# Attention scores as two products of 64 keys each, in a fused linear-attention and MLP kernel

## The chip, the cores and the metric

The kernel runs on one core of a Trainium2 chip. The core has five engines that run side by side: TensorE (PE; its weight loads are shown apart as PEld), VectorE (DVE), ScalarE (ACT), GpSimd (POOL) and SyncE (SP), which issues the DMAs here. The metric is the device time of one execution in microseconds, the median over runs; less is better.

## The reference, cut to what matters

A recurrence over 768 steps for 4 batches and 8 heads of width 48 with a complex, elementwise decay, and behind it a GELU MLP over all 3072 tokens:

```python
mag = np.sqrt(a_re * a_re + a_im * a_im)
scale = np.minimum(mag, 0.999) / (mag + 1e-06)
for t in range(S):
    new_re = ar * S_re - ai * S_im
    new_im = ar * S_im + ai * S_re
    S_re, S_im = (new_re + k_t v_t^T, new_im)
    y[:, :, t] = q_t @ S_re
...
h = x @ w_in            # 384 -> 2048
g = gelu(h)
return g @ w_out        # 2048 -> 384
```

## The kernel before, in words

**Lanes.** The products of the decays are made by a scan on DVE over 24 slices in four groups of positions (`GROUPS`: two of 2 x 64 positions, two of 2 x 128). Each slice is normalised (ACT and DVE, with `ident_r` sums on PE in the first slices), scanned (`tt`, `bt`), multiplied into k and q (`xt<-a,bt`) and written to DRAM (`kq<-xt`). A unit can load its part (`kqn<-kq`) when all slices of its group are written.

**Units.** There are 24 units of 128 positions of one batch, position by position: units 0 to 3 and 4 to 7 lie in the groups with chunks of 64 rows, units 8 to 23 in those with 128. A unit transposes k and q of four heads at a time (a half: `att<-ident_r,kqn`, copied to `kT` and `qT`), makes their scores (`scores`: `att<-qT,kp`, `kT` being the upper part of a `kp` tile), multiplies the scores by a causal mask on DVE (`kp<-att,causal`; for chunks of 64 the mask also blocks the earlier chunk), and makes `y` from them (`att<-kp,vn`), from the state before (`att<-qT,st`), and adds k^T v to the state (`att<-vn,kqn`). Then `x` and `xT` are split into a high and a low part (`minus`) and moved by DMA (`xT<-x`).

**Weights.** The weights come in 32 pieces as 64-bit floats (`raw`) and are converted to a high and a low part: on ACT and DVE (`wh`), and three products on PE (`po<-wh,ident_r`, then two with `minus`).

**Blocks.** Two or three units form one of nine blocks. Per block and each of 16 slices of the hidden width, `first` makes `ph` (nine products), ACT takes the GELU twice (`gf`, `gh`), DVE the difference (`gl`), and `second` adds to `po`.

**Order.** All of this is written to a list of steps, and a planner (`Plan`) puts every engine's instructions in one fixed order by estimated costs and by seven constants, `MORE`, which shift the priority of the kinds of work (lanes of each group, weights, units, blocks). Every instruction is then issued from line 393, so the groups of the profile are told apart by their tiles. PE products of 32-bit floats appear as two records in the trace, those with float32r operands as one.

`att` are three PSUM banks that transposes, scores and `y` take in turn.

Of the kernel before, what the change touches and what calls it, by code (L numbers as in the profile page):

```python
# [23 lines left out]
C = 128  # L24
# [36 lines left out]
def vap(t, dims):  # L61
    t = t[:] if not isinstance(t, bass.AP) else t
    return bass.AP(t.tensor, t.offset, [list(t.ap[0])] + dims)
# [28 lines left out]
N_A = 4  # L92
WL = 0.307

MORE = dict(lanes0=80.88, lanes1=16.18, lanes2=-95.71, lanes3=203.18, weights=-3.78, units=92.04, blocks=48.05)
BIAS = dict(vector=0.45, scalar=-0.29, gpsimd=0.38)


# [9 lines left out]
class Plan:  # L108
# [142 lines left out]
    def natural(self):  # L251
# [4 lines left out]
        for i in range(len(steps) - 1, -1, -1):  # L256
# [9 lines left out]
            rest[i] = t  # L266
        return [t + MORE[s.kind] for t, s in zip(rest, steps)]

# [135 lines left out]
def lanes_and_chunks(ctx, tc, flags, a_lanes, x_lanes, v_units, w_in, w_out, out):  # L404
    nc = tc.nc
# [4 lines left out]
    P = Plan(nc, loose=[flags])  # L410

    def ring(name, shape, n, dtype=F32, pool=cst):
        return itertools.cycle([pool.tile(shape, dtype, name=f"{name}{i}", tag=f"{name}{i}")[:] for i in range(n)])
# [44 lines left out]
    own = [ps.tile([128, 512], F32, name=f"att{i}", tag=f"att{i}")[:] for i in range(3)]  # L458
    ph = [ps.tile([128, 512], F32, name=f"ph{i}", tag=f"ph{i}")[:] for i in range(2)]
    pos = [ps.tile([128, 512], F32, name=f"po{i}", tag=f"po{i}")[:] for i in range(BLK)]  # L460
    ps_h = itertools.cycle(ph)
    raws = ring("raw", [128, DM * (2 if wide else 1)], N_RAW, w_in.dtype)
    whs = ring("wh", [128, DM], 2, U32)
# [277 lines left out]
    def unit(u):  # L741
# [3 lines left out]
        chunks, row = [], 0  # L745
# [80 lines left out]
        qT, kT, kp, pm = [], [], [], []  # L826
# [13 lines left out]
        def scores(hh):  # L840
            p = next(ps_att)
            with P.together():
                for j in range(4):
                    P.tensor.matmul(out=p[:, j * 128:(j + 1) * 128], lhsT=kT[hh][:, j, :], rhs=qT[hh][:, j, :], start=True, stop=True)
            t = kp[hh]
            P.vector.tensor_tensor(out=t, in0=p.rearrange("p (j l) -> p j l", j=4), in1=vap(masks[chunks[0][4]], [[0, 4], [1, 128]]), op=ALU.mult)
            pm.append(t)
# [17 lines left out]
        if early:  # L865
# [6 lines left out]
            for hh in range(2):  # L872
                turn(kn, kT, "kT", hh)
                turn(qn, qT, "qT", hh)
                scores(hh)
                y(hh)
                for c in with_state:
                    y_state(c, hh)
            for c in with_state:
                add_state(c, turned[c])  # L880
        else:
            for hh in range(2):
                turn(kn, kT, "kT", hh)
                turn(qn, qT, "qT", hh)
                scores(hh)
# [12 lines left out]
        j = next(j for j in range(len(BLOCKS)) if u < first_unit[j + 1])  # L898
# [238 lines left out]
def tile_complex_linear_attention_moe(ctx, tc, q, k, v, a_re, a_im, w_in, w_out, a_lanes, x_lanes, v_units, w_pieces, out):  # L1137
# [9 lines left out]
    with ExitStack() as fast:  # L1147
        fast.enter_context(tc.manual_schedule())
        lanes_and_chunks(fast, tc, flags, a_lanes, x_lanes, v_units, w_pieces, w_out, out)
# [81 lines left out]
```

## Time and profile before

| | before |
|---|---|
| median of 3 runs | 715.82 us (715.65 to 717.05) |
| span of the profiled execution | 713.3 us; the median run is 2.5 us longer |
| PE busy | 654.8 us (92%), 5190 matmul records |
| PE weight loads | 595.6 us (84%) |
| DVE, ACT, POOL busy | 456.6, 451.0, 52.6 us |
| chain that ended last, by engine | PE 65%, DVE 12%, ACT 11%, DMA 7% |

The span runs from the first to the last instruction; the time of a run holds some us around it. Busy times are sums of one engine's instructions, averaged over stages in which different engines wait for each other. PE's records overlap, so its work is read here from the start of one group to the start of the next.

### The profile page before, as it was taken

Reading aid. Unit: us, or ns where it says so; the run is one execution under the profiler, and the core shown is the slowest. Engines: PE = TensorE matmul, PEld = TensorE weight load, DVE = VectorE, ACT = ScalarE, POOL = GpSimd, SP = SyncE. Lnnn points to the kernel's source line nnn. Section 1 sums busy time; section 2 is a strip of 40 time slices with the busy share of each in tenths; the row PEclk is TensorE's granted clock in tenths of the full one; section 3 lists DMA queues with packets and bytes.
Section 4 is the critical chain, followed back from the end, with each engine's and each line's share of the span. In section 5 each row is a group of like instructions: output and inputs, shape, how many; then the busy total and the mean of one; then the engine's idle time right before and its main releaser. Section 6 shows DMA issues by size and latency. Waiting matters only on the chain.

```text
span 713.3 us, 13809 instructions
## 1 busy us (share of the span) xinstructions
PE 654.8 (92%) x5190; PEld 595.6 (84%) x5190; DVE 456.6 (64%) x1104; ACT 451.0 (63%) x1069; POOL 52.6 (7%) x85
## 2 busy tenths in 40 slices
PE   5635699997999999999999999999999999999995
PEld 2312478886889899989899999999999999999995
DVE  5999989997899999989999962433232221222211
ACT  8777779997688778887898864353433343343332
POOL 1002241003000200301010000100000000000000
PEclk9975599999999999999999999999999999999998
DMA  9357977668275566657586465032302112010000
GB/s 300 108 132 189 241 192 226 166 175 181 48 215 132 122 145 168 158 160 198 160 249 156 93 168 145 26 91 68 103 10 74 61 40 64 1 40 6 23 1 26
DMA packets 112840, 86.68 MB, mean 122 GB/s; under 512 B 55808, under 2 KB 105088, under 8 KB 112768
## 3 DMA queue, kind: packets, MB, share of 16 engines
q1 hardware_dynamic: 112768, 85.75, 44.9%
q8 instruction: 42, 0.69, 0.4%
q14 instruction: 30, 0.25, 0.1%
HBM read 56.82 MB, written 23.59 MB: 113 GB/s over the span
## 4 chain that ended last, share of the span: by engine, by line
PE 65%; DVE 12%; ACT 11%; DMA 7%; SPq 2%; issue 2%; DVEq 0%; ACTq 0%
PE po L393 23%; PE ph L393 23%; PE att L393 19%; DVE a L393 3%; DMA m<-st 3%; SPq L393 2%; ACT a L393 2%; ACT tab L393 2%; ACT wh L393 2%; DMA kqn<-kq 2%; DVE tt L393 2%; DVE tab L393 1%; DVE xt L393 1%; ACT L391 1%; DMA xt<-in_x_lanes_dram 1%
## 5 line engine op out<-in xcount | busy, mean ns | idle before, releaser
L393 PE MATMUL ph<-xT,wi_hi 128*128 128x384 f32 (+1 forms) x864 | 211.5, 326 | 0.0
L393 DVE TENSOR_TENSOR gl<-gf,gh 128x384 fp32r<-128x384 f32 (+1 forms) x141 | 72.2, 512 | 168.0 <-ACT gf L393 165.1
L393 PEld LDWEIGHTS ph<-xT,wi_hi 128*128 128x128 f32 x864 | 153.1, 189 | 3.6 <-issue 1.6
L393 ACT ACTIVATE gh<-ph 128x384 fp32r<-128x384 f32 (+1 forms) x144 | 65.7, 456 | 129.4 <-PE ph L393 129.1
L393 PE MATMUL ph<-xT,wi_lo 128*128 128x384 f32 (+1 forms) x432 | 137.5, 318 | 0.0
L393 PE MATMUL po<-wo_hi,gh 128*128 128x384 f32 x384 | 132.9, 346 | 1.7 <-ACT gh L393 1.4
L393 PE MATMUL po<-wo_lo,gh 128*128 128x384 f32 x384 | 129.8, 338 | 0.0
L393 PE MATMUL po<-wo_hi,gl 128*128 128x384 f32 x384 | 93.8, 345 | 0.0
L393 PEld LDWEIGHTS ph<-xT,wi_lo 128*128 128x128 f32 x432 | 81.7, 189 | 0.0
L393 PEld LDWEIGHTS po<-wo_hi,gh 128*128 128x128 f32 x384 | 72.2, 188 | 5.0 <-ACT gh L393 3.4
L393 PEld LDWEIGHTS po<-wo_lo,gh 128*128 128x128 f32 x384 | 72.5, 189 | 0.1
L393 DVE TENSOR_TENSOR tt<-bt,a 128x192 f32<-128x192 f32 x192 | 68.3, 356 | 1.2
L393 PEld LDWEIGHTS po<-wo_hi,gl 128*128 128x128 f32 x384 | 65.4, 189 | 1.6 <-issue 0.9
L393 ACT ACTIVATE gf<-ph 128x384 f32<-128x384 f32 (+1 forms) x144 | 65.3, 453 | 0.7 <-DVE gl L393 0.5
L393 PE MATMUL att<-qT,kp 96*128 96x128 f32 x384 | 52.2, 279 | 1.5 <-DVE kp L393 1.5
L393 PEld LDWEIGHTS att<-qT,kp 96*128 96x128 f32 x384 | 48.4, 192 | 3.8 <-ACT a L393 2.1
L393 DVE TENSOR_TENSOR bt<-tt 128x96 f32<-128x96 f32 x192 | 49.2, 256 | 1.1
L393 PE MATMUL po<-wh,ident_r 128*128 128x384 f32 x64 | 33.7, 615 | 15.5 <-DVE wh L393 6.9
L393 DVE TENSOR_TENSOR kp<-att,causal 128x512 f32<-128x512 f32 x48 | 33.0, 687 | 19.0 <-PE att L393 18.1
L393 PE MATMUL att<-ident_r,kqn 128*96 128x128 f32 x384 | 38.5, 240 | 5.2 <-DMA kqn<-kq 4.4
L393 ACT COPY kp<-att 96x512 f32<-96x512 f32 x47 | 27.3, 582 | 24.4 <-PE att L393 23.8
L393 PEld LDWEIGHTS att<-ident_r,kqn 128*96 128x96 f32 x384 | 33.9, 128 | 9.3 <-issue 5.6
(177 smaller groups left out, 1018.1 us busy)
## 6 DMA issues: line engine op xcount, KB each, us to landing
kqn<-kq SPq DMA_DIRECT2D x16, 768.0 KB, 5.4
xt<-in_x_lanes_dram SPq DMA_DIRECT2D x24, 384.0 KB, 4.5
kq<-xt SPq DMA_DIRECT2D x24, 384.0 KB, 4.1
kq<-xt SPq DMA_DIRECT2D x48, 192.0 KB, 4.5
a<-in_a_lanes_dram SPq DMA_DIRECT2D x20, 384.0 KB, 3.3
raw<-in_w_pieces_dram SPq DMA_DIRECT2D x16, 384.0 KB, 4.1
raw<-in_moe_w_out_dram SPq DMA_DIRECT2D x16, 384.0 KB, 4.5
vn<-in_v_units_dram SPq DMA_DIRECT2D x24, 256.0 KB, 5.1
```

What stands on the lines that cost most here:

```text
L391: self.nc.scalar.preload_act_table_set(table)
L393: getattr(getattr(self.nc, engine), name)(*args, **kw)
```

## The change

The four 128 x 128 score products of a half become eight: for each head the keys 0 to 63 against all queries of the chunk and the keys 64 to 127 against the queries 64 to 127. For chunks of 64 rows the lower keys meet the queries 0 to 63 alone. The part of the bank that is no longer written is masked to zero afterwards; so that it holds finite numbers the three `att` banks are cleared at the start. Four of the seven planner constants are moved by more than 1.

```diff
-MORE = dict(lanes0=80.88, lanes1=16.18, lanes2=-95.71, lanes3=203.18, weights=-3.78, units=92.04, blocks=48.05)
+MORE = dict(lanes0=60.85, lanes1=16.18, lanes2=-77.98, lanes3=203.18, weights=-44.11, units=115.14, blocks=47.55)
...
     pos = [ps.tile([128, 512], F32, name=f"po{i}", tag=f"po{i}")[:] for i in range(BLK)]
+    for p in own:
+        nc.vector.memset(p, 0.0)
...
                 for j in range(4):
-                    P.tensor.matmul(out=p[:, j * 128:(j + 1) * 128], lhsT=kT[hh][:, j, :], rhs=qT[hh][:, j, :], start=True, stop=True)
+                    for k0 in (0, 64):
+                        k1 = k0 + 64 if k0 or chunks[0][4] == 64 else C
+                        P.tensor.matmul(out=p[k0:k0 + 64, j * 128 + k0:j * 128 + k1], lhsT=kT[hh][:, j, k0:k0 + 64],
+                                        rhs=qT[hh][:, j, k0:k1], start=True, stop=True)
```

In the planner a product with at most 64 stationary columns has the form "narrow", with a cost of its own and a cost for changes of form, so the scores change their form there, too.

PE's order at unit 20, before: the first half's scores (four products of 128 x 128), then transposes of the second half, and later the second half's scores and the first `y`.

```order
L393 MATMUL ph_112<-xT_149,wi_lo 128x384
L393 MATMUL att_108<-qT_144,kp_146 128x128 x4
L393 MATMUL att_109<-ident_r,kqn_139 96x128 x4
L393 MATMUL att_110<-ident_r,kqn_139 96x128 x4
L393 MATMUL ph_112<-xT_149,wi_hi 128x384 x2
...
L393 MATMUL po_115<-wo_lo,gh_155 128x384
L393 MATMUL att_108<-qT_145,kp_147 128x128 x4
L393 MATMUL att_109<-kp_146,vn_141 64x128 x4
L393 MATMUL po_113<-wo_hi,gl_157 128x384
```

The same place of the change, where each "..." inside a half stands for the pair of rows above it, three times more:

```order
L393 MATMUL po_115<-wo_lo,gh_159 128x384
L393 MATMUL att_108<-qT_147,kp_149 64x128
L393 MATMUL att_108<-qT_147,kp_149 64x64
...
L393 MATMUL att_109<-ident_r,kqn_142 96x128 x4
L393 MATMUL att_110<-ident_r,kqn_142 96x128 x4
L393 MATMUL po_113<-wo_hi,gl_161 128x384
...
L393 MATMUL ph_112<-xT_152,wi_lo 128x384
L393 MATMUL att_108<-qT_148,kp_150 64x128
L393 MATMUL att_108<-qT_148,kp_150 64x64
...
L393 MATMUL att_109<-kp_149,vn_144 64x128 x4
L393 MATMUL ph_112<-xT_152,wi_hi 128x384 x2
```

The first half's scores are now a group of their own with 64 stationary columns between groups with 128 and 96; the second half's are joined to the `y` product that has 64 as well.

SP's order (DMA issues) around the first loads of units 4 and 5, before: `raw` are weight pieces, `kq` the last writes of group 1, `kqn` the units' loads, each "x2" the two chunks of 64 rows.

```order
L393 DMA raw_118<-in_w_pieces_dram 128x768
L393 DMA raw_119<-in_moe_w_out_dram 128x768
L393 DMA a_125<-in_a_lanes_dram 128x2x384
L393 DMA kq_105<-xt_131 64x8x192
L393 DMA kq_105<-xt_131 64x8x96 x2
L393 DMA kq_105<-xt_132 64x8x192
L393 DMA kq_105<-xt_132 64x8x96 x2
L393 DMA xT_149<-x_150 16x256 x6
L393 DMA xt_131<-in_x_lanes_dram 128x8x96
L393 DMA kqn_139<-kq_105 64x8x192 x2
L393 DMA kqn_140<-kq_105 64x8x192 x2
```

And in the change:

```order
L393 DMA kq_105<-xt_135 64x8x192
L393 DMA kq_105<-xt_135 64x8x96 x2
L393 DMA vn_145<-in_v_units_dram 128x512
L393 DMA raw_121<-in_w_pieces_dram 128x768
L393 DMA raw_122<-in_moe_w_out_dram 128x768
L393 DMA kqn_142<-kq_105 64x8x192 x2
L393 DMA kqn_143<-kq_105 64x8x192 x2
L393 DMA raw_119<-in_w_pieces_dram 128x768
L393 DMA xT_152<-x_153 16x256 x4
L393 DMA raw_120<-in_moe_w_out_dram 128x768
```

The loads of units 4 and 5 had all 32 weight pieces ahead of them; four pieces stand behind them now.

## Rows read from the trace of the kernel before

**Rows 1.** The page's head and PE's line of its busy times: busy us (share of the span) x instructions.
```profile
span 713.3 us, 13809 instructions
...
PE 654.8 (92%) x5190; PEld 595.6 (84%) x5190; DVE 456.6 (64%) x1104; ACT 451.0 (63%) x1069; POOL 52.6 (7%) x85
```

**Rows 2.** Busy time of each engine in four stages: stretch, its length, busy us (x instructions) by engine, then granted clock of TensorE, DMA share and GB/s.
```profile
core 0: us, PE busy (x) PEld busy (x) DVE busy (x) ACT busy (x) POOL busy (x), PEclk, DMA share, GB/s
0.00:85.00 85.00, 44.71 (x97) 22.49 (x99) 73.28 (x201) 64.65 (x158) 8.80 (x30) 0.77 0.70 194
85.00:175.00 90.00, 84.56 (x802) 71.85 (x800) 82.41 (x210) 81.71 (x213) 19.66 (x19) 0.97 0.71 188
175.00:425.00 250.00, 244.99 (x2153) 227.74 (x2154) 230.13 (x558) 199.40 (x416) 20.42 (x26) 0.99 0.61 155
425.00:640.00 215.00, 215.00 (x1666) 209.28 (x1664) 56.97 (x102) 82.87 (x216) 3.74 (x11) 1.00 0.21 62
```

**Rows 3.** PE's waits between 175 and 425 us: who waited for whom, us in total, times, longest.
```profile
PE att L393 <- DMA kqn<-kq: 4.4, 1, 4.4
PE att L393 <- DVE kp L393: 2.7, 4, 1.0
PE att L393 <- ACT kp L393: 0.8, 1, 0.8
```

**Rows 4.** PE in order of time around a half's scores that stand between full-array groups (unit 18): start us, us, engine, line, operation, out<-in, stationary rows*columns, shape, count of records.
```profile
502.49 0.52 PE L393 MATMUL ph<-xT,wi_hi 128*128 128x384 f32 x2
502.84 0.34 PE L393 MATMUL ph<-xT,wi_lo 128*128 128x384 f32 x1
...
503.54 1.05 PE L393 MATMUL att<-qT,kp 96*128 96x128 f32 x8
504.35 0.77 PE L393 MATMUL att<-ident_r,kqn 128*96 128x128 f32 x8
504.95 0.58 PE L393 MATMUL ph<-xT,wi_hi 128*128 128x384 f32 x2
505.37 0.33 PE L393 MATMUL ph<-xT,wi_lo 128*128 128x384 f32 x1
```

**Rows 5.** The same view at unit 20's `y` and state products, which have 64 and 48 stationary columns.
```profile
558.75 0.66 PE L393 MATMUL att<-kp,vn 128*64 128x128 f32 x8
559.34 0.78 PE L393 MATMUL po<-wo_hi,gl 128*128 128x384 f32 x3
...
560.30 0.34 PE L393 MATMUL ph<-xT,wi_lo 128*128 128x384 f32 x1
560.57 0.66 PE L393 MATMUL att<-kp,vn 128*64 128x128 f32 x8
561.06 1.05 PE L393 MATMUL att<-qT,st 96*48 96x128 f32 x16
562.03 0.62 PE L393 MATMUL ph<-xT,wi_hi 128*128 128x384 f32 x2
562.49 0.34 PE L393 MATMUL ph<-xT,wi_lo 128*128 128x384 f32 x1
562.67 0.34 PE L393 MATMUL po<-wo_hi,gh 128*128 128x384 f32 x1
```

**Rows 6.** The same view at state products with 64 moving columns.
```profile
232.38 0.65 PE L393 MATMUL att<-qT,st 96*48 96x64 f32 x16
232.97 0.62 PE L393 MATMUL ph<-xT,wi_hi 128*128 128x384 f32 x2
```

**Rows 7.** Instructions that read or write `kp`: count, duration in ns as min/median/max, first and last start, forms.
```profile
L393 PE MATMUL att<-qT,kp x384: 272/275/488, 89.8 to 639.1; 96*128 96x128 f32 x192
...
L393 PE MATMUL att<-kp,vn x352: 271/273/324, 112.2 to 640.8; 128*64 128x128 f32 x176
L393 DVE TENSOR_TENSOR kp<-att,causal x48: 672/691/693, 91.1 to 639.5; 128x512 f32<-128x512 f32 x48
```

**Rows 8.** PE in order of time: a weight piece (three groups, the first and the last shown by their starts) and the start of unit 4; in brackets the idle time before and its releaser.
```profile
160.62 0.81 PE L393 MATMUL po<-wh,ident_r 128*128 128x384 f32 x2
...
161.62 0.51 PE L393 MATMUL po<-wo_hi,gl 128*128 128x384 f32 x2
161.97 0.40 PE L393 MATMUL ph<-xT,wi_hi 128*128 128x256 f32 x2
...
176.15 1.06 PE L393 MATMUL att<-ident_r,kqn 128*96 128x128 f32 x8 [4.39 <-DMA kqn<-kq]
```

**Rows 9.** Busy time from 85 to 175 us of the instructions that read or write `wh` alone: length, PE, PEld, DVE, ACT (x instructions), clock, DMA share, GB/s. A piece has two such records on PE, three instructions on DVE and five on ACT.
```profile
85.00:175.00 90.00, 14.59 (x34) 5.63 (x34) 23.59 (x51) 29.36 (x82) 0.97 0.71 188
```

**Rows 10.** SP's DMA issues in order of time ahead of unit 4's load.
```profile
156.83 7.07 SPq L393 DMA_DIRECT2D kq<-xt  x6
164.01 4.28 SPq L393 DMA_DIRECT2D xT<-x  x6
...
168.97 2.66 SPq L393 DMA_DIRECT2D kqn<-kq  x4
```

**Rows 11.** DVE's first instruction.
```profile
6.65 0.36 DVE L393 TENSOR_SCALAR wh<-raw 128x384 uint32<-128x384 uint32 x1 [6.65 <-ACT wh L393]
```

**Rows 12.** All engines in order of time, of which the load and the first transposes of unit 8.
```profile
301.33 1.00 SPq L393 DMA_DIRECT2D kqn<-kq  x2
...
308.29 0.69 PE L393 MATMUL att<-ident_r,kqn 128*96 128x128 f32 x8
```

**Rows 13.** A row of the page's DMA issues: count, KB each, median us from issue to landing.
```profile
kqn<-kq SPq DMA_DIRECT2D x16, 768.0 KB, 5.4
```

## The prediction

> **What bounds the kernel now.** I read the stages first. Up to 85 us no engine carries the kernel: PE works off weight pieces while the lanes of group 0 run on DVE and ACT. From 85 to 175 us three engines are near full: PE 84.56, DVE 82.41 and ACT 81.71 of 90 us [rows 2]. From 175 to 425 PE has 244.99 of 250, DVE 230.13; from 425 to 640 PE has 215.00 of 215 at a granted clock of 1.00, and DVE and ACT are mostly idle [rows 2]. A busy PE could still be a waiting one, so I read its waits next: between 175 and 425 us they are 4.4 us for `kqn<-kq`, 2.7 for DVE and 0.8 for ACT, and nothing else of size [rows 3]. So from unit 4's first transposes at 176.15 [rows 8] PE works through its order without a pause for the remaining 537 us of the span of 713.3 [rows 1]. What the change does to the sum of PE's pitches (from the start of one group to the start of the next) reaches the end, less what happens before 176 us.
>
> **What PE pays now for scores.** A half is eight full-array records. It starts at 503.54, the transposes behind it at 504.35: 0.81 us. The records overlap with what follows, and the next group pays for it: the transposes take 0.60 to 504.95. A plain transpose run costs 0.53 to 0.54 (0.60 less the 0.07 to 0.08 that any group pays behind such a run: `ph` x2 takes 0.42 at 504.95 where it takes 0.35 at 502.49) [rows 4]. So a half costs 0.81 + 0.08 = 0.89, and 48 halves cost 42.7 us.
>
> **What a 64-column product costs.** Products with 64 or fewer stationary columns are in the program already (`att<-kp,vn`, `att<-qT,st`). Sixteen records, eight products, with 128 moving columns take 561.06 to 562.03, 0.97 us; 0.10 of it is the way out (below), so 0.87 / 8 = 0.109 each [rows 5]. With 64 moving columns eight products take 232.38 to 232.97, 0.59; less 0.05 in and 0.10 out, 0.055 each [rows 6].
>
> **What a run of them costs besides.** Going into one, `ph` x1 takes 0.27 (560.30 to 560.57) and not 0.18 (562.49 to 562.67): +0.09. The first four products take 0.49, where four in the middle take 0.44: +0.05. Four that end the run take 0.59 (558.75 to 559.34) and not 0.49: +0.10. The `ph` x2 behind it takes 0.46 (562.03 to 562.49) and not the 0.35 of rows 4: +0.11 [rows 5, 4]. The toll is 0.35 us for each run, however short.
>
> **How many runs.** I counted them in both orders, a run being neighbours on PE with at most 64 stationary columns. Before there are 60, the scores among none of them. After there are 86: 20 consist of scores alone, 28 mix scores with `y` or state products. Transpose runs go from 63 to 73. The example of unit 20 shows it: scores that stood between full-array groups at no toll become two runs of their own kind, one alone, one joined to `kp,vn`. The 26 added runs cost 26 x 0.35 = 9.1 us, ten transpose runs 10 x 0.08 = 0.8.
>
> **What the new products cost.** The eight units with 64-row chunks (16 halves) get 64 x 64 products: 8 x 0.055 = 0.44 a half, 7.0 us. The other 32 halves have, per head, one product of 128 moving columns for the lower key half and one of 64 for the upper. No row shows such an unequal pair. Lower bound: they take their 0.109 and 0.055 one behind the other, 4 x 0.164 = 0.66 a half. Upper bound: the longer product of each pair sets the pace. The rows say something on this. A record of `att<-kp,vn` lasts 273 ns, a full-array record of `att<-qT,kp` 275 [rows 7]. A narrow record is therefore no quicker than a full one; eight full ones take 0.81 us, and sixteen narrow ones 0.87. That is two narrow ones in the time of one, side by side. Wherever this kernel issues them, they alternate between the lower and the upper output half (`h % 2 * 64`, `c0`) with equal lengths. If the two halves of the output are what runs side by side, a lower product of 128 beside an upper one of 64 leaves the upper half idle, and a head costs two equal products, 2 x 0.109: 4 x 0.218 = 0.87 a half. I take 0.87, because the equal record times are what side by side looks like and a cheaper product isn't.
>
> The Trainium skill, page TensorEngine Tiling (Array Packing), section Key Properties, says that different tiles of the array can load weights and multiply in parallel. No run here shows an unequal pair; by that rule the upper bound would hold, and the sum would be the one I take, where by the products' own rows added up it would be the lower bound's.
>
> **The sum on PE.** After: 7.0 + 32 x 0.87 + 9.1 + 0.8 = 44.7 against 42.7, +2.1 us with the fractions kept. With 0.66 for the wide halves: 7.0 + 21.1 + 9.1 + 0.8 = 38.0, -4.7.
>
> **The stage before 176 us.** The three memsets on DVE write 128 x 512 PSUM words each; the nearest row, a DVE pass over such a bank, takes 0.69 [rows 7], together 2.1 at most. DVE's first instruction of before starts at 6.65 after 6.65 of waiting [rows 11]: free; without that cover 2.1. The new table moves weight pieces behind the lanes of group 1. In SP's order the four `kqn` loads of units 4 and 5 have no piece behind them before, and four `raw` loads after; on PE 31 of the 32 pieces stand ahead of unit 4's first transposes before, 26 after. A piece takes 1.0 us of PE (160.62 to 161.62) [rows 8]; on ACT 29.36 us over some 16.5 pieces, 1.8, and on DVE 23.59 over 17, 1.4, without the casts of `lo` [rows 9]. Five fewer pieces take 8.9 off ACT and 6.9 off DVE, the two engines on which the lanes of group 1 run, and both are nearly full there. I let unit 4's `kqn` land 9 us earlier than the 176 of before. PE has 5.0 less in pieces ahead of it, four fewer groups each of block 0's `ph`, `wo_hi,gh` and `wo_lo,gh` and two fewer `gl` (3.2, at 0.175 per 384 columns, from 161.62 to 161.97 for two) [rows 8], and about 1.5 less for the eight halves of units 0 to 3 (7.1 before; 3.5 and six tolls after): 9.7. PE so arrives 9.7 earlier for a load that comes 9 earlier, and the wait of 4.4 becomes about 5. I take +1.0, with bounds of -4.4 (the pieces kept for later fill the wait) and +4.4 (the lanes gain half of it only). `kqn` in turn waits behind `kq<-xt` and the `xT<-x` on SP, 156.83 to 168.97 [rows 10]; the new order has two `raw` loads there and no `xT<-x`, which I cost at nothing, since the wait is for `kq` to land.
>
> Pieces moved behind 176 us add 7 to DVE in a stage where it has 230 of 250: still under its room of 20, so PE stays the bound. **Sum:** 713.3 + 2.1 + 1.0 = 716.4 span. The median run of 715.82 is 2.5 longer than the span shown; I keep that: **718.9**.
>
> **Rivals.**
> *Narrow products are simply cheaper.* The wide halves cost 0.66, PE's sum falls by 4.7, and with the +1.0 ahead the time is 715.8 - 3.7 = 712.1, faster. For it: the two prices of rows 5 and 6 follow moving columns exactly (0.109 and 0.055). Against: the equal record times of rows 7. It decides from a wide half under 0.78 on (41.7, which is 42.7 less the 1.0, = 7.0 + 9.9 + 32 x 0.775).
> *The wait at unit 4 closes.* The pieces left over give PE work while `kqn` lands; 4.4 goes and the +1.0 with it: 718.9 - 5.4 = 713.5. For it: five pieces of 1.0 are there to fill it. Against: PE takes its order as it stands, and the pieces stand behind the transposes.
> *A later unit waits.* Unit 8's `kqn` is issued at 301.33, a load takes 5.4 to land, and its transposes start at 308.29 [rows 12, 13]: about 1 us to spare. If the lanes of group 2 come later than that against PE, a wait of the kind of rows 8 appears: up to 4.4, giving 723.3.
>
> **Chances.** The forecast 0.45, cheaper products 0.22, the closed wait 0.13, the later wait 0.20. A change under 0.2% (1.4 us) can't be told from none in this kernel. Faster by more: 0.22 and over half of 0.13, 0.30; within: 0.17, from the low edge of the forecast and the rest of the closed wait; slower: 0.53. The range, 710.5 to 723.5, takes in cheaper products and the later wait; cheaper products with the wait closed too (706.7) lie outside. The forecast's own range is 717 to 721.
>
> **What would show it.** In the changed kernel a wide half with its 16 records should take about 0.87 us to the next group within a run, and 64 x 64 halves 0.44; 0.66 for the wide ones proves me wrong. Waits of PE behind 175 us should stay under 10 us, with one at unit 4 near 167 us. The stage from 425 us to the end, where PE alone counts, should hold more PE time per unit than before. The forecast fails if the wide half is cheap, if the wait for `kqn` goes, or if DVE becomes PE's releaser between 175 and 425.

## The result and the profile after

| | before | changed |
|---|---|---|
| median | 716.43 us (715.65 to 717.19, 4 runs) | 726.98 us (720.77 to 730.44, 4 runs) |
| ratio, 95% interval | | 1.0142 (1.0104 to 1.0180) |
| span of the profiled execution | 713.3 us | 725.7 us (its time: 727.38) |

The change is slower by 10.5 us. The direction was forecast, the size was not: 718.9 was the forecast, 723.5 the upper end of the range. Where a run was disturbed the comparison leaves it out, so a ratio below can differ from that of the medians beside it.

The head of the page of the changed kernel:

```profile
span 725.7 us, 14647 instructions
...
PE 660.7 (91%) x5574; PEld 589.3 (81%) x5574; DVE 458.8 (63%) x1099; ACT 456.4 (63%) x1090; POOL 70.8 (10%) x95
```

The four stages of [rows 2], with the same columns (busy us of PE, PEld, DVE, ACT, POOL; granted clock, DMA share, GB/s):

```profile
0.00:85.00 85.00, 44.03 (x118) 22.98 (x118) 76.20 (x209) 64.37 (x157) 7.03 (x29) 0.73 0.70 196
85.00:175.00 90.00, 83.27 (x857) 69.43 (x856) 75.10 (x189) 74.78 (x191) 17.99 (x18) 0.89 0.73 183
175.00:425.00 250.00, 240.40 (x2294) 217.63 (x2290) 232.68 (x561) 204.13 (x443) 40.57 (x37) 0.99 0.61 154
425.00:640.00 215.00, 215.00 (x1744) 203.61 (x1743) 58.34 (x106) 85.75 (x219) 5.17 (x12) 1.00 0.22 62
```

Two rows stand out against [rows 2]. From 85 to 175 us the granted clock fell from 0.97 to 0.89. From 175 to 425 us PE has 4.6 us less busy time. The last stage is as full as before. DVE and ACT have 7 us less busy time from 85 to 175 us, but that is work that went elsewhere: the weight pieces (`wh`) alone take 8.0 us less of DVE and 6.6 less of ACT there than in [rows 9]:

```profile
85.00:175.00 90.00, 11.30 (x24) 4.15 (x24) 15.64 (x37) 22.73 (x62) 0.89 0.73 183
```

A busy PE hides two things, so I took PE's records apart: for each kernel the sum of all pitches (start to next start) at full clock, which is PE's **work**; the time in which no record ran, **idle**; and what the half clock added, which is half of PE's running time where the granted clock is 0.50. Counted is from unit 0's first transposes to PE's last record, cut at unit 4's first transposes:

| us | unit 0 / unit 4 at | to unit 4: work, idle, half clock | from unit 4: work, idle, half clock |
|---|---|---|---|
| before | 86.3 / 176.2 | 81.7, 6.6, 1.6 | 522.8, 4.8, 2.7 |
| changed | 85.2 / 170.1 | 69.9, 6.7, 8.3 | 535.7, 10.6, 2.5 |

PE's whole work rose by 1.1 us (604.5 to 605.6). The loss is elsewhere: 5.9 us of idle time and 6.6 of half clock. With the 1.1 of work, and less 1.1 by which unit 0 came earlier, they make the 12.4 us of the span.

Not all of the half clock lies behind the two stops below. Of the 8.3 us, 3.8 stand ahead of 94 us, where the clock comes to full at 93.7 us and not at 89.4 as before (1.6 us there). The stretch from 89 to 94 us, changed first:

```profile
89.00:94.00 5.00, 5.00 (x33) 3.81 (x32) 3.84 (x7) 2.47 (x6) 0.00 (x0) 0.53 0.79 241
```
```profile
89.00:94.00 5.00, 5.00 (x63) 4.30 (x61) 3.64 (x9) 4.23 (x10) 0.00 (x0) 0.96 1.03 292
```

All traces with the order of the change have this late rise, at 93.5 to 96.6 us, also those of kernels that lost nothing; no run was made on it.

**The products** cost about what the forecast took. PE in order of time, a wide half by itself (start, us, engine, line, operation, out<-in, stationary rows*columns, shape of the first record, count of records):

```profile
353.22 0.34 PE L393 MATMUL ph<-xT,wi_lo 128*128 128x384 f32 x1
353.49 1.09 PE L393 MATMUL att<-qT,kp 96*64 96x128 f32 x16
354.50 0.62 PE L393 MATMUL ph<-xT,wi_hi 128*128 128x384 f32 x2
354.96 0.33 PE L393 MATMUL ph<-xT,wi_lo 128*128 128x384 f32 x1
...
102.94 0.66 PE L393 MATMUL ph<-kp,vn 128*64 128x128 f32 x8
103.42 0.64 PE L393 MATMUL att<-qT,kp 96*64 96x64 f32 x16
103.89 0.39 PE L393 MATMUL ph<-qT,st 96*48 96x64 f32 x8
```

From 353.49 to 354.50 are 1.01 us: 0.87 within rounding, and the 0.15 that a run of narrow products pays inside it; `ph` x2 behind it takes the 0.46 of [rows 5]. The short half between other narrow products takes 0.47, where 0.44 was forecast.

**The first stop.** PE around 116 us (the bracket is the idle time ahead and its releaser), then the granted clock (third figure from the end of a row) in pieces of 2 us:

```profile
115.52 0.81 PE L393 MATMUL att<-m,other_half 96*128 96x384 f32 x2
118.77 0.77 PE L393 MATMUL ph<-xT,wi_hi 128*128 128x256 f32 x2 [2.44 <-DMA xT<-x]
```
```profile
116.00:118.00 2.00, 0.33 (x2) 0.00 (x0) 1.99 (x7) 1.97 (x6) 0.00 (x0) 0.89 0.44 154
118.00:120.00 2.00, 1.23 (x6) 1.26 (x7) 2.00 (x8) 0.59 (x2) 1.33 (x1) 0.50 0.20 37
120.00:122.00 2.00, 2.00 (x23) 1.63 (x22) 0.64 (x3) 0.00 (x0) 1.49 (x1) 0.50 0.96 286
122.00:124.00 2.00, 2.00 (x35) 1.91 (x33) 0.00 (x0) 1.32 (x6) 0.00 (x0) 0.50 0.23 91
...
128.00:130.00 2.00, 2.00 (x30) 1.71 (x28) 1.18 (x3) 1.42 (x4) 0.00 (x0) 1.00 0.10 25
```

PE waits 2.4 us for the DMAs of `xT`, the clock falls to 0.50 (1.2 GHz) for some 10 us, and PE's products take about double there: `ph` x2 0.77 us where it took 0.40 in [rows 8]. DVE and ACT stop with it (DVE 0.00 busy from 122 to 124 us), because copies of PE's results stand at the head of their queues. Their waits from 115 to 130 us (who for whom, us, times, longest):

```profile
DVE xT L393 <- PE att L393: 5.4, 1, 5.4
```
```profile
ACT xT L393 <- PE att L393: 3.5, 1, 3.5
```

The same 15 us of both kernels, changed first:

```profile
115.00:130.00 15.00, 12.55 (x104) 10.35 (x103) 8.73 (x26) 8.97 (x24) 2.82 (x1) 0.66 0.47 142
```
```profile
115.00:130.00 15.00, 15.00 (x175) 12.41 (x173) 14.78 (x41) 14.17 (x42) 1.05 (x1) 1.00 0.62 188
```

DVE and ACT have 6.1 and 5.2 us less busy time there, of which the waits shown are 5.4 and 3.5, and the lanes of group 1 run on them. What is late next is unit 4: its load is issued at 162.96 and its transposes start at 170.09.

**The second stop.** SP, then ACT, then PE around 396 us, and the clock:

```profile
389.30 2.28 SPq L393 DMA_DIRECT2D m<-st  x2
```
```profile
396.76 1.91 ACT L393 ACTIVATE m<-m,gg 96x48 f32<-96x48 f32 x8 [4.07 <-DMA m<-st]
398.57 0.56 ACT L393 COPY qT<-att 96x512 f32<-96x512 f32 x1
```
```profile
395.14 0.41 PE L393 MATMUL att<-ident_r,kqn 128*96 128x128 f32 x4
399.19 0.66 PE L393 MATMUL att<-ident_r,kqn 128*96 128x128 f32 x4 [3.63 <-ACT qT L393]
```
```profile
397.00:400.00 3.00, 0.81 (x7) 0.68 (x9) 0.00 (x0) 3.00 (x11) 0.00 (x0) 0.58 0.96 201
400.00:404.00 4.00, 4.00 (x24) 3.23 (x24) 2.11 (x5) 3.98 (x13) 0.99 (x1) 0.50 0.65 152
404.00:406.00 2.00, 2.00 (x41) 1.83 (x41) 0.33 (x1) 1.94 (x4) 0.00 (x0) 0.93 0.00 0
```

The eight products of unit 15's state with its gains (`m<-m,gg`) wait on ACT for a DMA that was issued at 389.30. Behind them in ACT's queue stands the copy of unit 14's `qT`, whose transposes started at 393.24; PE's next transposes need its bank. PE stands for 3.6 us and then works at half clock until 404. That the order alone makes this stop is what state_move_later tests below.

### The profile page after: what moved, and what is told of

Read it like the earlier page. It is cut to its first block, busy times and chain, and to the rows that moved or that the text cites. A ratio compares the mean times of both kernels' runs of the same rounds, so it can differ in the third digit from the quotient of the medians.

```text
span 725.7 us, 14647 instructions
## 1 busy us (share of the span) xinstructions
PE 660.7 (91%) x5574; PEld 589.3 (81%) x5574; DVE 458.8 (63%) x1099; ACT 456.4 (63%) x1090; POOL 70.8 (10%) x95
## 4 chain that ended last, share of the span: by engine, by line
PE 65%; DVE 11%; DMA 10%; ACT 9%; issue 2%; SPq 2%; DVEq 0%; ACTq 0%
PE po L393 25%; PE ph L393 25%; PE att L393 15%; DMA kq<-xt 3%; DMA m<-st 2%; DVE a L393 2%; SPq L393 2%; DMA kqn<-kq 2%; ACT a L393 2%; DVE tab L393 1%; ACT tab L393 1%; DVE tt L393 1%; ACT wh L393 1%; DVE xt L393 1%; DMA vn<-in_v_units_dram 1%
## 5 line engine op out<-in xcount | busy, mean ns | idle before, releaser
L393 DVE TENSOR_TENSOR tt<-bt,a 128x192 f32<-128x192 f32 x192 | 70.9, 370 | 1.0
L393 DVE TENSOR_TENSOR bt<-tt 128x96 f32<-128x96 f32 x192 | 50.8, 264 | 0.8
L393 PE MATMUL att<-qT,kp 96*64 96x64 f32 (+1 forms) x768 | 46.6, 252 | 0.6 <-ACT qT L393 0.6
L393 PEld LDWEIGHTS att<-qT,kp 96*64 96x64 f32 x768 | 37.3, 140 | 7.7 <-issue 2.5
L393 PEld LDWEIGHTS po<-wh,ident_r 128*128 128x128 f32 x64 | 12.5, 229 | 25.2 <-ACT wo_lo L393 9.9
```

Of the source, the lines that this page charges most:

```text
L393: getattr(getattr(self.nc, engine), name)(*args, **kw)
```

## The experiments

Theory O: the products were priced rightly, and the loss comes from the new order (two stops, the half clock behind them, work moved behind unit 4). Its rivals are named with each run. All edits are to the changed kernel unless the text says otherwise.

| kernel | median us (range, runs) | before beside it | ratio (interval) |
|---|---|---|---|
| split_in_old_order | 718.55 (716.56 to 719.89, 10) | 716.20 | 1.0038 (1.0010 to 1.0065) |
| full_in_new_order | 723.05 (721.98 to 725.53, 4) | 716.20 | 1.0119 (1.0070 to 1.0167) |
| split_old_table | 723.46 (719.77 to 726.98, 4) | 715.81 | 1.0104 (1.0052 to 1.0156) |
| full_new_table | 724.43 (722.83 to 725.52, 4) | 715.81 | 1.0116 (1.0075 to 1.0158) |
| change_again | 722.69 (722.27 to 725.13, 5) | 714.55 | 1.0121 (1.0094 to 1.0147) |
| first_stop_only | 721.04 (716.34 to 722.48, 6) | 714.55 | 1.0083 (1.0055 to 1.0111) |
| state_move_later | 719.07 (716.84 to 722.13, 10) | 716.20 | 1.0045 (1.0015 to 1.0076) |
| state_move_and_piece_later | 716.63 (714.25 to 725.76, 10) | 716.20 | 1.0016 (0.9989 to 1.0043) |
| pe_stop_filled | 714.52 (713.50 to 718.44, 4) | 715.81 | 0.9990 (0.9944 to 1.0036) |
| split_short_units | 726.01 (715.44 to 732.41, 4) | 715.81 | 1.0024 (0.9957 to 1.0091) |
| split_where_free | 712.03 (709.77 to 713.36, 7) | 715.23 | 0.9951 (0.9932 to 0.9970) |
| old_order_split_where_free | 712.89 (709.62 to 716.11, 12) | 715.23 | 0.9965 (0.9949 to 0.9981) |

### The products without the order, the order without the products

The planner's order of one kernel is kept and only what is issued for the scores is exchanged. split_in_old_order, in the kernel before (with the clears):

```diff
             t = kp[hh]
+            P.steps[-1].real = [("tensor", "matmul", (), dict(out=p[k0:k0 + 64, j * 128 + k0:j * 128 + k1], lhsT=kT[hh][:, j, k0:k0 + 64],
+                                                             rhs=qT[hh][:, j, k0:k1], start=True, stop=True))
+                                for j in range(4) for k0 in (0, 64) for k1 in (k0 + 64 if k0 or chunks[0][4] == 64 else C,)]
...
-            for engine, name, args, kw in s.calls:
+            for engine, name, args, kw in s.real or s.calls:
```

> The kernel before with its order kept step for step; only what is issued for a half's scores is changed to the eight smaller products (and the three banks are cleared at the start). Theory O (order): the products cost what the forecast took (0.87 us for a wide half, 0.44 for a half of 64-row chunks, 0.35 for each run of narrow products); counted in this order PE's sum is 2.4 us over before, so 717 to 720 us, with no new wait of PE over 2 us behind unit 4. Theory P (products): the loss of some 10 us is in the products or the clears themselves; then this kernel shows most of it, 724 us or more.

Measured: 718.55 us; PE's work is 606.2, 1.7 over before where 2.4 was worked out. Unit 4 still waits:

```profile
175.62 1.06 PE L393 MATMUL att<-ident_r,kqn 128*96 128x128 f32 x8 [4.49 <-DMA kqn<-kq]
```

The products and the clears together cost some 2.4 us. Theory P falls.

full_in_new_order is the reverse, four full products issued in the steps of the changed kernel.

> The changed kernel with its order kept step for step, but the scores issued as four full products a half. Theory O: PE's sum is 4.6 us over that of the changed kernel (full products dearer in this order), the two stops of PE near 116 and 396 us and the half clock behind them stay; 726 to 733 us, slower than before by 10 or more. Theory P: without the split products the loss goes; 714 to 719 us.

Measured: 723.05 us. PE's work is 609.6, 4.0 over the changed kernel where 4.6 was expected, so in this order the split products are the cheaper ones. But the time is 3 us under the expected range. One row shows why. The second stop is there:

```profile
398.00 0.47 PE L393 MATMUL att<-ident_r,kqn 128*96 128x128 f32 x4 [3.35 <-ACT qT L393]
```
```profile
385.00:405.00 20.00, 16.65 (x130) 15.33 (x126) 15.31 (x41) 15.96 (x42) 2.03 (x2) 1.00 0.66 168
```

but the granted clock stays at 1.00 around it, and at 119.78 PE waits 0.5 us for `xT` instead of 2.4, being later itself. The half clock costs 6.1 us in all, not some 11. The loss stays without the split products. But of the 8.6 us that this trace is longer than that of before, 5.1 are PE's work, 2.0 idle time and 1.8 half clock: most of it is here the price of full products in an order made for split ones. So this run does not show what the stops cost; the next ones do.

### The two stops taken away

state_move_later moves one step on ACT, state_move_and_piece_later one more on SP, pe_stop_filled three more on PE. `shift` puts the steps of its second argument behind those of its third: unit 15's products `m` behind unit 14's last copy of `kp` and `qT`; the load of `raw` ahead of unit 1's `xT` behind the six DMAs of that; block 0's first three groups of `ph` behind unit 2's `att<-vn,kqn`.

```diff
+        order = self.order()
+        seq = [s for s in order if s.engine == "scalar"]
...
+        order = self.shift(order, [seq[m[0]]], [seq[c[-1]]])
+        seq = [s for s in order if s.engine == "sync"]
...
+        order = self.shift(order, [seq[raw]], [seq[x[-1]]])
+        seq = [s for s in order if s.engine == "tensor"]
...
+        order = self.shift(order, seq[i:j], [seq[k - 1]])
-        for s in self.order():
+        for s in order:
```

> The changed kernel with one step moved on ACT: the eight products of unit 15's state with its gains, which wait for a DMA until 396.8 us, stand behind the four copies of unit 14's transposes and no longer ahead of three of them. Theory O: PE's stop of 3.6 us for that copy goes, and with it the 7 us at half clock behind it (3.5 us of work): about 7 us faster than the changed kernel's profiled run, 718 to 722 us. Rival L (lanes): PE would have met a later wait anyway, since unit 16's load comes at 438.7 us; then the gain is under 3 us, 724 us or more, with a wait for kqn at unit 16.

Measured: 719.07 us. Around the place where PE stood (with the transposes in one group of eight records):

```profile
394.97 0.69 PE L412 MATMUL att<-ident_r,kqn 128*96 128x128 f32 x8
395.59 0.65 PE L412 MATMUL att<-qT,kp 96*64 96x128 f32 x10
```
```profile
385.00:405.00 20.00, 20.00 (x204) 18.56 (x200) 17.95 (x48) 18.25 (x45) 2.96 (x2) 1.00 0.72 177
```

No stop, full clock, and 7 us won by the ratios (1.0142 to 1.0045), or 5.5 if the change is taken by its other runs (1.0121, change_again); the intervals lie apart either way. In the traces PE's idle time behind unit 4 falls from 10.6 to 4.7 us and its half clock from 2.5 to none. Rival L falls: no later wait took it back.

> The same, and on SP one weight piece's load is put behind the six DMAs of unit 1's xT, so that these are issued 1.7 us earlier (112.4 instead of 114.2 us). Theory O: PE's stop of 2.4 us for xT at 116.3 us falls to under 1 us; if the clock then stays at full, the 10 us of half clock from 117 us go too, DVE and ACT (8.7 and 9.0 busy of 15 us from 115 to 130 us) wait less for PE, and unit 4's load is issued 3 to 6 us before 163.0: 712 to 717 us. Rival H (hidden): PE has slack before unit 4, whose load sets the end of this stage; then nothing comes of it beyond the first move, 718 to 722 us.

Measured: 716.63 us, 2.4 less, with intervals that overlap. The stop became 2.0 us, not under 1 (the six DMAs took 5.7 us to issue), and a stretch at half clock from 120.5 to 127.4 us stayed. The profiled run was one of the longer ones (719.33 us), so its trace does not show what the others gained.

> The kernel with the state step and the weight piece moved, and on PE the three groups of block 0's first slice, which wait for xT at 118 us, put behind the next two groups of unit 2 (state products and k times v, some 3 us of work at full clock). Theory O: PE's stop of 2.0 us goes and the 8 us at half clock behind it; DVE's and ACT's waits for PE there (ACT 2.6 us) go, and unit 4's load is issued 3 us earlier or more: 711 to 715 us. Rival H (hidden): unit 4's load is set by the lanes alone; 715.5 to 718 us.

Measured: 714.52 us. PE has work in the place of the stop, at full clock; DVE and ACT have 13.0 and 13.7 of the 15 us again; unit 4's load is issued at 157.78, 5.2 us earlier than in the change, and PE starts on it at 164.82:

```profile
117.06 0.65 PE L421 MATMUL att<-qT,st 96*48 96x64 f32 x16 [0.65 <-DVE st L421]
117.65 1.13 PE L421 MATMUL att<-vn,kqn 64*64 64x48 f32 x32
118.71 0.50 PE L421 MATMUL ph<-xT,wi_hi 128*128 128x256 f32 x2
...
164.82 0.73 PE L421 MATMUL att<-ident_r,kqn 128*96 128x128 f32 x8 [1.43 <-DMA kqn<-kq]
```
```profile
115.00:130.00 15.00, 13.89 (x153) 11.87 (x154) 12.97 (x37) 13.66 (x37) 3.55 (x2) 1.00 0.58 174
```
```profile
157.78 2.65 SPq L421 DMA_DIRECT2D kqn<-kq  x4
```

So PE's half clock ahead of unit 4 was not hidden by the lanes; it slowed them. Five steps moved on three engines took the loss away: the interval of the ratio, 0.9944 to 1.0036, takes in 1. What the last three add to the two before them lies within the noise of the times; the traces show it, unit 4 starting at 164.82 and not at 169.72.

first_stop_only has the moves on SP and PE alone.

> The changed kernel with the weight piece and the three groups of block 0's first slice moved, but the state step of unit 15 left where the change has it. Theory O: unit 4's transposes start near 165 us and no longer at 170, the stop of 3.6 us near 391 us and what follows it stay: 4 to 6 us under the changed kernel, 720 to 723 us, and some 7 us over the kernel with all three steps moved. Rival: with PE earlier at that place the stop grows by what was gained, 725 us or more.

Measured: 721.04 us, 1.7 us under the changed kernel run beside it (2.7 by the ratios, whose intervals overlap): less than expected. Unit 4 did start at 164.1, 3.2 us before change_again's. The six runs lie in two clusters, 716.3 and 717.7, and 720.2 to 722.5. The profiled one is the 716.3: its stop for `qT` was 1.4 us with 3.4 us at half clock. I did not trace one of the others, so where they lost the rest stays open. Of the two stops only the second is shown to cost time by a run that takes it away alone; what the first costs is read from the traces.

> The changed kernel itself, unaltered, on the same chip as the run beside it, to have more of its runs: 724 to 730 us by the theory that its two stops come back in nearly every run; were the first four runs (720.8 to 730.4 us) an accident, 717 to 721 us.

Measured: 722.69 us, 8.1 over before on the same chip; the loss is no accident, but smaller than in the first four runs. Both stops are back (2.49 and 3.22 us); at the first one only 3.4 us ran at half clock (119.5 to 122.9 us), where the first profile had 10, and unit 4 started 2.8 us earlier than there:

```profile
167.31 0.73 PE L393 MATMUL att<-ident_r,kqn 128*96 128x128 f32 x8 [0.98 <-DMA kqn<-kq]
...
393.47 0.66 PE L393 MATMUL att<-ident_r,kqn 128*96 128x128 f32 x4 [3.22 <-ACT qT L393]
```

The spans of the two profiled executions of this kernel are 5.0 us apart: 3.4 us of idle time and 1.9 of half clock, with the same stops. What moved the other runs, from 720.8 to 730.4 us, was not traced.

### Each part of the change alone, ordered anew

split_old_table and full_new_table exchange the one line, in the changed kernel and in the one before:

```diff
-MORE = dict(lanes0=60.85, lanes1=16.18, lanes2=-77.98, lanes3=203.18, weights=-44.11, units=115.14, blocks=47.55)
+MORE = dict(lanes0=80.88, lanes1=16.18, lanes2=-95.71, lanes3=203.18, weights=-3.78, units=92.04, blocks=48.05)
```

> The split scores and the clears with the constants of before; the planner makes a new order from them. 31 weight pieces stand ahead of unit 4's transposes, as before, and the narrow products form 101 runs (60 before, 86 in the change); by the prices of the forecast PE's sum is 7.8 us over before. Theory O (products priced right, the rest is order): 721 to 727 us, with unit 4's wait for kqn still there near 176 us. Theory P' (the constants are what hurts): 714 to 718 us.

Measured: 723.46 us, PE's work 611.6, 7.1 over before (7.8 worked out). Theory P' falls.

> The full scores of before with the constants of the change; the planner makes a new order from them. 24 pieces stand ahead of unit 4's transposes; 82 narrow runs and 48 halves at full price put PE's sum 9.1 us over before. Theory O: 721 to 730 us; the constants are worth nothing without the split scores. Theory P' predicts a loss as well, but the same as in the change, 725 to 728 us, with stops of PE like those at 116 and 396 us; Theory O puts most of the loss in PE's work, at least 6 us over before from 85 us on.

Measured: 724.43 us, PE's work 611.4, 6.9 over before (9.1 worked out).

Each part alone is about as slow as both together, for another reason: with the old constants the split scores make 101 narrow runs, with the new ones 86. By the counts, the new constants save tolls; the stops came with their order.

split_short_units has the constants of before and splits in units 0 to 7 alone:

```diff
-                    for k0 in (0, 64):
+                    for k0 in (0, 64) if chunks[0][4] == 64 else (0,):
+                        if chunks[0][4] == C:
+                            P.tensor.matmul(out=p[:, j * 128:(j + 1) * 128], lhsT=kT[hh][:, j, :], rhs=qT[hh][:, j, :], start=True, stop=True)
+                            continue
...
```

> The constants of before, with the split only in the eight units whose chunks have 64 rows (both products of a head 64 x 64); the other sixteen keep the full products. PE's sum is 1.0 us under before by the prices. Half of the halves lie ahead of unit 4's wait, where PE has slack. Theory O: 714 to 718 us, not to be told from before. Any result over 721 us would mean that a new order alone costs several us, whatever the products.

Measured: a ratio of 1.0024, with 1 inside its interval, 0.9957 to 1.0091. PE's work is 603.2, 1.3 under before where 1.0 was worked out. Its profile has a stop and a half clock of its own:

```profile
226.74 1.12 PE L393 MATMUL att<-qT,kp 96*64 96x64 f32 x16 [3.41 <-DVE kp L393]
```
```profile
223.00:233.00 10.00, 6.59 (x97) 5.56 (x94) 7.65 (x18) 5.16 (x11) 2.04 (x2) 0.66 0.35 86
```

It decides nothing on the split; its profile is one more new order with a stop that nobody planned.

### Splitting only where it is free

A split half of a short unit saves PE time anywhere; a wide one (0.87 against 0.89) only if it adds no run. split_where_free does this on top of pe_stop_filled:

```diff
+        for was, s, then in zip(seq, seq[1:], seq[2:]):
+            if s.full and "narrow" not in (was.form, then.form):
+                s.calls = s.full
...
```

> The kernel with the three steps moved; besides, 17 of the 32 wide halves, those with no other narrow product next to them on PE, are issued as four full products again. By the prices of the forecast each of the 17 saves its toll of 0.35 us less 0.02 for its products: PE's sum 5.7 us lower, all of it behind unit 4. Theory O: 708 to 710 us, faster than both kernels. Rival: the lanes or a later load take PE's gain back; 712 us or more, with a wait for kqn behind 300 us.

Measured: 712.03 us, faster than before by 0.5% and than the change by 1.7 to 1.9%, but 2 us over what was expected. PE's work is 601.6, 4.2 lower than in pe_stop_filled and not 5.7, and 1.7 us came back as a half clock at unit 4's wait. Behind 200 us PE has no wait for `kqn`, so the rival's mechanism is not there.

old_order_split_where_free keeps the order of before and exchanges what is issued:

```diff
+            if s.split and (s.short or "narrow" in (was.form, then.form)):
+                s.calls = s.split
...
```

> The order of before, step for step; split are the 16 halves of the units with 64-row chunks and the 9 wide halves that stand next to another narrow product, the other 23 are full. PE's sum is 5.3 us under before, 3.3 of it ahead of unit 4's transposes, where the wait for kqn of 4.4 us takes it up. Theory O: 2 us faster than before, 713 to 715.5 us. Rival: the 3.3 us count as well, 710 to 712 us.

Measured: 712.89 us, 2.3 less than before beside it (2 worked out); PE's work is 600.1, 4.4 lower, 2.0 of it ahead of unit 4, whose transposes start at 175.0 behind a wait of 4.3 us, as before. What PE gains ahead of a wait is largely lost in it.

## Why the prediction was wrong

**Right: the price of the products.** The wide half at 0.87, the toll and PE's sum (+1.1 us, forecast +2.1) stand; the short half takes 0.47 and not 0.44. The rival "simply cheaper" needed a wide half of 0.66, and no row shows it: the 64-column product hides beside the 128-column one. The rule of the Trainium skill, page TensorEngine Tiling (Array Packing), section Key Properties, that tiles multiply in parallel, agrees with this trace: a head's pair takes 0.218 us, as two products with 128 moving columns do, and not the 0.164 of its two rows added up.

**Right: the clears are free.** In the trace of the change they run on DVE from 1.01 to 2.58 us, and the first `wh` behind them starts at 6.72 where it started at 6.65 [rows 11].

**Wrong, the first step that failed: "I let unit 4's `kqn` land 9 us earlier".** The load came 6.0 us earlier (168.97 in [rows 10], 162.96 after), and unit 4 started at 170.09, where the forecast's "near 167" was meant. The step counted the pieces taken off DVE and ACT and took it that they would use the time. They waited instead, for a PE at half clock. With that stop filled the load came at 157.78 us, 11.2 earlier than before: the 9 us were there, and more. How much this step misses changes from one execution to the next: in change_again, with 3.4 us at half clock, the load came at 160.47 and unit 4 started at 167.31, as forecast.

**Wrong, the second, and in both traces of the change: "PE stays the bound" behind 176 us at no cost.** DVE's room was judged rightly (232.68 of 250 us). What failed is that only load was looked at. The stop came from ACT, which had 46 us to spare in that stage, since a step that waits for a DMA stood ahead of one that PE needed. Idle time behind unit 4 rose from 4.8 to 10.6 us (8.4 in change_again), of which this stop is 3.6 (3.2); state_move_later shows 5.5 to 7 us for this one place, with the half clock behind it.

**The rival "a later unit waits" was of the right kind, and missed its place and price.** It looked at unit 8's load alone, and allowed 4.4 us for the wait and nothing for the clock behind it. Yet before had this in its own trace: unit 4's wait of 4.4 [rows 8] is followed by transposes of 1.06 us where 0.69 is usual [rows 12]. A stop of PE could have been priced at its length and up to 5 us more, half of the 3.4 to 10.2 us at half clock seen behind stops here.

In sum, against the forecast's span of 716.4: unit 4 later than forecast 2.6, more work behind it 1.1 (12.9 against 11.8), more idle time there 5.8, a little less half clock there 0.2: the 725.7 of the trace. The time outside the span was 1.7 us, not 2.5.

That the kernel came out slower, as forecast, was partly luck: of the 12.4 us the forecast's own ground for it, more work on PE, gives 1.1; the rest is idle time and half clock, to which it gave at most the longer wait at unit 4, and that wait got shorter (1.7 us, not 5).

## What to carry to other kernels

When a change makes a planner or a scheduler lay out a new order, price the order as well as the operations: look in the order for every step that waits for a DMA with another engine's next step queued behind it. To tell the two apart, keep the order and exchange the operations, and the reverse; then take each time apart into work, idle time and half clock, since an order made for one kind of product can make the other dearer. Use a smaller product only where it joins a run of its kind, and where PE has no wait ahead that swallows the gain.

## What the runs showed of the hardware

A product with 64 stationary and 64 moving columns costs PE nothing beside one with 64 and 128 on the other half of the output: sixteen records take 0.87 us, as with all of 128.

From unit 0 on, the 14 traces have 29 stops of PE of 1.4 us or more that began at full clock. Behind 18 of them the granted clock fell to 0.50 for 3.4 to 10.2 us, behind 11 it did not, and their length alone does not part the two kinds: stops of 1.41 us (first_stop_only) and 1.60 (split_short_units) had such a stretch behind them, stops of 2.32 (split_short_units) and 3.35 (full_in_new_order) had none. The same kernel had 10.2 us behind its first stop in one execution and 3.4 in another. The Trainium skill, page TensorE: Matmul & The Clock Gate, section HAM oscillation — how this bites in real kernels, tells of waits for DMA after which PE starts again at the lower clock. The 18 agree with it (not all of them waits for DMA), the 11 do not; and these traces add that engines which copy PE's results wait with it (behind one stop DVE had 6.1 and ACT 5.2 us less busy time in 15).
